# Lending two PSUM banks to the convolution inside a saturated TensorE stream

## The chip, the cores and the metric

The kernel runs on one core of one Trainium2 chip, as one launch. The metric is the device time of that launch in microseconds, lower is better. Five engines work side by side, each through its own queue in order: PE (TensorE, the matmuls), DVE (VectorE), ACT (ScalarE), POOL (GpSimd) and SP (which here only issues DMAs). Matmul results land in PSUM, which has eight banks of 128 partitions x 512 float32; ACT or DVE must copy a result out before the bank is filled again.

## The reference

What is computed is the forward pass and all gradients of a sum of two branches on a normalised input. Cut to what matters:

```python
x  = A_q                       # 1 x 2048 x 1024, bf16
xn = layernorm(x)
# branch A: short convolution of k (4 taps), times v, long convolution over
# 2048 steps with ssm_k by FFT of length 4096, plus kv * ssm_D, times q = xn
# branch B: h = relu(xn @ W_gate) * (xn @ W_up);  out = h @ W_down   (F = 3584)
out = x + A(xn, k, v, shift_k, ssm_k, ssm_D) + B(xn, W_gate, W_up, W_down)
# outputs: out, and by vjp with grad_out: the gradients of q, k, v, shift_k,
# ssm_k, ssm_D, W_gate, W_up, W_down
```

## The kernel before

Branch B is all dense 128x128 matmuls with 512 columns, and they come in three stages:

1. *hidden*: for each half of the rows and each block of 512 columns of F, per row tile a gate product (`ps_g`), an up product (`ps_u`) and a gradient product (`ps_h`), 8 matmuls each, into one bank each.
2. *weight gradients*: `grad_down` (`ps_d`) and `grad_in` (`ps_w`), 16 matmuls to a product.
3. *output*: `ps_o`, `ps_x` and a rest `ps_r`.

Branch A, the convolution, is done for eight groups of 128 channels. Its FFT is split into small matmuls on tiles of 32x64 or 64x32 of the array, and their passes are put between the dense products of stages 1 and 2. A generator of steps, `slots`, says what each slot holds: a pass on PE (left) and a piece of DVE work (right). Every pass writes tiles of two banks each, from a pool of two tiles, and ACT copies each tile to SBUF (`act`).

```python
self.ps = self.pool("a_ps", 2, space=PSUM)          # branch A: 2 tiles of 2 banks

def fwd2(self, F, half):                             # 64x32 step, filter
    for j0 in range(0, 4, 2):
        for j in range(j0, j0 + 2):
            ps = self.ps.tile([P, 2, 2, 2, 2, 64], F32, name="ps2", tag="aps")
            ...                                      # 32 matmuls of 128 columns
            self.act(F[:, 2 * j:2 * j + 2]..., ps[:]...)
        yield                                        # a pass: two tiles

def fwd2_pair(self):                                 # 64x32 step, both spectra
    for j in range(4):
        ps = [self.ps.tile(...) for _ in range(2)]
        ...                                          # 32 matmuls of 256 columns
        yield                                        # a pass: two tiles

SLOT, DENSE = 1900, (1900, 1250)
A_START = 45_000
# cut: slots(); in it, for one group
#   yield f2, None  x4, with a slot without a pass between them
#   ... yield f2H, tg ; yield f2H, fly ; yield self.inv_b(st, "yt", 0), flh ...
```

Branch B has the other four banks. Each product takes the next of four one-bank tiles:

```python
self.ps = tc.alloc_tile_pool(name="b_ps", bufs=4, space=PSUM)

def ps_tile(self, name):
    return self.ps.tile([P, 512], F32, name=name, tag="bps")

# hidden: who empties the bank
def gate(s, held=False):
    ps = self.ps_tile("ps_g"); self.gemm8(ps, xT[s], wg)
    nc.scalar.activation(out=ru[s][:, 0, :], in_=ps[:], func=ACT.Relu)
def up(s, mid=None, after={}, put=..., hold=False):
    ps = self.ps_tile("ps_u"); self.gemm8(ps, xT[s], wu, mid, after)
    def masked():
        nc.vector.scalar_tensor_tensor(out=ru[s][:, 1, :], in0=ru[s][:, 0, :],
                                       scalar=0.0, in1=ps[:], ...)
    ...
def grad_row(s, mid=None):
    ps = self.ps_tile("ps_h"); self.gemm8(ps, gT[s], wd, mid)
    nc.scalar.copy(out=gh[:], in_=ps[:])

# first rows: up(0) is broken off after 4 matmuls for the rows 1 to 3,
# and its masked() is held back until the middle of up(2)
gate(0); up(0, None, {3: first_mid}, lambda *fs: held.extend(fs), True)

# weight gradients: one product of 16 matmuls
def gemm16(self, ps, lhsT, rhs):
    for st in range(self.ST):
        matmul(ps[:], lhsT=lhsT(st), rhs=rhs(st), start=(st == 0), stop=(st == self.ST - 1))
        if st % 8 == 7:
            yield 1730                               # a slot of branch A may come here
            self.tick()
# and after it: nc.scalar.copy(out=wo[0][:, ob, :], in_=ps[:])
```

Three times in stage 2 four products are open at once (`four`: the first blocks of `grad_down` and `grad_in` and one late in `grad_down`), which takes all four banks.

Of the kernel before, what the change touches and what calls it, by code (L numbers as in the profile page):

```python
# [17 lines left out]
P = 128  # L18
# [27 lines left out]
NB1 = 32  # L46


class ABranch:
# [5 lines left out]
    def __init__(self, tc, pri, S, D, k, v, g, shift_k, ssm_k, ssm_D, xn_d, y_d, sk_d, out_gk, out_gv, out_gsk,  # L55
                 out_gh, out_gsD):
        assert S == 2048 and D % P == 0
        self.tc, self.nc, self.pri = tc, tc.nc, pri
        self.S, self.D, self.NG = S, D, D // P
        self.k, self.v, self.g, self.shift_k, self.ssm_k, self.ssm_D = k, v, g, shift_k, ssm_k, ssm_D  # L60
        self.xn_d, self.y_d, self.sk_d = xn_d, y_d, sk_d
        self.out_gk, self.out_gv, self.out_gsk, self.out_gh, self.out_gsD = out_gk, out_gv, out_gsk, out_gh, out_gsD
        self.pools, self.pin, self.dense, self.queue = [], False, False, []

    def pool(self, name, bufs, **kw):
        p = self.tc.alloc_tile_pool(name=name, bufs=bufs, **kw)
        self.pools.append(p)
        return p

# [260 lines left out]
    def fwd1_filter(self, st):  # L330

        B, hn = self.Bh, st["hn"]
        for k in range(2):
            for x in range(2):
                ps = self.ps.tile([P, 2, 512], F32, name="ps0", tag="aps")
                for b in range(2):
                    rows = slice(64 * x + 32 * b, 64 * x + 32 * b + 32)
                    for h in range(2):
                        self.mm(ps[64 * h:64 * h + 64, b], self.R[rows].rearrange("p a l -> p (a l)"),
                                hn[rows, h, 16 * k:16 * k + 16, :].rearrange("p c n -> p (c n)"))  # L340
                self.act(B[:, :, x, 8 * k:8 * k + 8],
                         ps[:].rearrange("p b (cp i n) -> p b cp n i", i=2, n=NB1))
            yield
# [7 lines left out]
    def fwd1(self, B, src):  # L351
        for r0 in range(0, 16, 8):
            for u in range(2):
                ps = self.ps.tile([P, 2, 8, 64], F32, name="ps1", tag="aps")
                for b in range(2):
                    rows = slice(64 * u + 32 * b, 64 * u + 32 * b + 32)
                    for h in range(2):
                        self.mm(ps[64 * h:64 * h + 64, b], self.R[rows].rearrange("p a l -> p (a l)"),
                                src[rows, r0:r0 + 8, 64 * h:64 * h + 64])
                self.act(B[:, :, :, u, r0:r0 + 8, :], ps[:].rearrange("p b r (cp i) -> p b cp r i", i=2))  # L360
            yield

    def fwd2(self, F, half):
        Bf = self.flp[:, half]
        for j0 in range(0, 4, 2):
            for j in range(j0, j0 + 2):
                ps = self.ps.tile([P, 2, 2, 2, 2, 64], F32, name="ps2", tag="aps")
                for ri in range(2):
                    for m in range(2):
                        for q in range(4):  # L370
                            for e in range(2):
                                rows, l = slice(64 * e, 64 * e + 64), 8 * q + 2 * j + m
                                self.mm(ps[32 * q:32 * q + 32, e, :, ri, m, :], self.FW[rows, l, ri, :],
                                        Bf[rows, l, :].rearrange("p (b c) -> p b c", b=2))
                self.act(F[:, 2 * j:2 * j + 2].rearrange("p e b i c -> p (e b i c)"),
                         ps[:].rearrange("p e b i m c -> p (e b i m c)"))
            yield

    def fwd2_pair(self):

        for j in range(4):
            ps = [self.ps.tile([P, 2, 2, 2, 2, 64], F32, name="ps2", tag="aps") for _ in range(2)]
            for m in range(2):
                for ri in range(2):
                    for q in range(4):
                        for e in range(2):
                            rows, l = slice(64 * e, 64 * e + 64), 8 * q + 2 * j + m
                            self.mm(ps[e][32 * q:32 * q + 32, m, :, :, ri, :], self.FW[rows, l, ri, :],
                                    self.flp[rows, :, l, :].rearrange("p k (b c) -> p b k c", b=2))
            for e in range(2):  # L390
                self.act(self.GK[:, 2 * j + e].rearrange("p b k i (m c) -> p (b k i) m c", m=2),
                         ps[e][:].rearrange("p m b k i c -> p (b k i) m c"))
            yield

# [26 lines left out]
    def inv_a(self):  # L421
        C, Q = self.Cg, self.GKV
        for j0 in range(0, 4, 2):
            ps = [self.ps.tile([P, 2, 2, 2, 2, 64], F32, name="ps3", tag="aps") for _ in range(2)]
            for j in range(2):
                for m in range(2):
                    for ri in range(2):
                        for q in range(4):
                            for e in range(2):
                                rows, x = slice(32 * q, 32 * q + 32), 2 * (j0 + j) + m  # L430
                                self.mm(ps[q // 2][64 * e:64 * e + 64, q % 2, j, m],
                                        self.IA[rows, x, ri].rearrange("p a n -> p (a n)"),
                                        Q[rows, 2 * (j0 + j) + e, :, ri, 64 * m:64 * m + 64],
                                        start=ri == 0, stop=ri == 1)
            for h in range(2):
                self.act(C[:, :, 2 * h:2 * h + 2, 2 * j0:2 * j0 + 4, :],
                         ps[h][:].rearrange("p q j m b (cp i) -> p (b cp) q (j m) i", i=2))
            yield

    def inv_a_pair(self):  # L440

        for j in range(4):
            ps = [self.ps.tile([P, 2, 2, 2, 2, 64], F32, name="ps3", tag="aps") for _ in range(2)]
# [9 lines left out]
            for h in range(2):  # L453
                self.act(self.Cs[:, :, 2 * h:2 * h + 2, 2 * j:2 * j + 2, :],
                         ps[h][:].rearrange("p q m k b (cp i) -> p (k b cp) q m i", i=2))
            yield

    def inv_b(self, st, key, half):
        dst, Cf = self.ttile(key), self.flp[:, half]
        st[key] = dst  # L460
        for j in range(2):
            ps = self.ps.tile([P, 2, 8, 64], F32, name="ps4", tag="aps")
            for q in range(4):
                for e in range(2):
# [4 lines left out]
                     ps[:].rearrange("p h r c -> p r h c"))  # L469
        yield  # L470

    def inv_b_chan(self, st, half):
# [3 lines left out]
        for n0 in range(0, NB1, 16):  # L476
            ps = self.ps.tile([P, 16, 64], F32, name="ps5", tag="aps")
            for n in range(16):
                self.mm(ps[:, n, :], Cf[:, n0 + n, :], self.RB[:].rearrange("p h n -> p (h n)"))
            self.act(dv[:, :, n0:n0 + 16], ps[:].rearrange("p n2 n1 -> p n1 n2"))  # L480
# [17 lines left out]
    def tap_sums(self, st):  # L498

        gks, kp = st["gks"], st["kp"]  # L500
        ps = self.ps.tile([P, 2, 512], F32, name="ps6", tag="aps")
        pd = ps[:, 0, 0:P].rearrange("p (i c) -> p i c", i=4)
# [11 lines left out]
    def both(self, *fs):  # L514
# [3 lines left out]
        return go  # L518

# [11 lines left out]
    def steps(self):  # L531
# [25 lines left out]
        for st in self.sts:  # L557
            for p, d in self.slots(st, st["gi"]):
                self.run(p)
# [198 lines left out]

    def small_outputs(self):
# [17 lines left out]
A_START = 45_000  # L777


class LnMlp:  # L780
# [7 lines left out]
    def open_left(self):  # L788
# [6 lines left out]
        self.ps = tc.alloc_tile_pool(name="b_ps", bufs=4, space=bass.MemoryType.PSUM)  # L795
# [38 lines left out]
    def ps_tile(self, name):  # L834
        return self.ps.tile([P, 512], F32, name=name, tag="bps")
# [184 lines left out]
    def flip_xn(self, st):  # L1020
        xT = self.act_tile("xnT", st)
        h = self.DT // 2 if st < 3 else self.DT
        for k0 in range(0, self.DT, h):
            pst = self.ps.tile([P, self.DT, P], BF16, name="pst_x", tag="bps")
# [21 lines left out]
    def hidden(self, first, goT, load, ln, tables, Wg, Wu, Wd, g, xn_d, h_d, ug_d):  # L1046
# [6 lines left out]
        for n in range(N):  # L1053
# [43 lines left out]
            def up(s, mid=None, after={}, put=lambda *fs: [f() for f in fs], hold=False):  # L1097
                ps = self.ps_tile("ps_u")
# [22 lines left out]
            def first_rows():  # L1121
# [16 lines left out]
                def last_mid():  # L1138
                    flip(4)
                    for f in held[0:2]:  # L1140
                        f()
                    chunk(1)
# [174 lines left out]
    def gemm16(self, ps, lhsT, rhs):  # L1317
        for st in range(self.ST):
            self.pri.pin(self.nc.tensor.matmul(ps[:], lhsT=lhsT(st), rhs=rhs(st), start=(st == 0),  # L1319
                                               stop=(st == self.ST - 1)))  # L1320
            if st % 8 == 7:
# [41 lines left out]
    def grad_down(self, xn_d, ug_d, h_d, out_wd):  # L1363
# [9 lines left out]
        for fb in range(self.FB):  # L1373
# [5 lines left out]
            for j in range(4):  # L1379
                self.pri.now()  # L1380
                if j - 1 in whole:
                    continue
                if j in whole:
                    wo = [self.e2_tile("wo") for _ in range(2)]
                    yield from self.four("ps_d", lambda i, st: hs(st)[:, (j + i // 2) * P:(j + i // 2 + 1) * P],
                                         lambda i, st: gn[st][:, i % 2 * 512:i % 2 * 512 + 512],
                                         lambda i: wo[i // 2][:, i % 2, :], load_xn if fb else none)
                else:
                    wo = [self.e2_tile("wo")]
                    for ob in range(2):  # L1390
                        ps = self.ps_tile("ps_d")
                        yield from self.gemm16(ps, lambda st: hs(st)[:, j * P:(j + 1) * P],
                                               lambda st: gn[st][:, ob * 512:ob * 512 + 512])
                        self.pri.pin(nc.scalar.copy(out=wo[0][:, ob, :], in_=ps[:]))
# [8 lines left out]
    def grad_in(self, ug_d, out_wg, out_wu):  # L1403
        nc, xn, nxt = self.nc, self.xn_nat, self.ugs
        turns = [(fb, w) for fb in range(self.FB) for w in (1, 0)]
        for k, (fb, w) in enumerate(turns):
# [3 lines left out]
            for dp in range(self.DT // 2):  # L1410
# [6 lines left out]
                if k == 0 and dp == 0:  # L1417
                    wo = [self.e2_tile("wi") for _ in range(2)]
                    yield from self.four("ps_w", lambda i, st: xn[st][:, i * P:(i + 1) * P], lambda i, st: sl(st),
                                         lambda i: wo[i // 2][:, i % 2, :], lambda st: None)  # L1420
                else:
                    wo = [self.e2_tile("wi")]
                    for d in range(2):
                        dc = 2 * dp + d
                        ps = self.ps_tile("ps_w")
                        yield from self.gemm16(ps, lambda st: xn[st][:, dc * P:(dc + 1) * P], sl)
                        self.pri.pin(nc.scalar.copy(out=wo[0][:, d, :], in_=ps[:]))
# [90 lines left out]
    def grad_x(self, x, g, xn_d, y_d, h_d, ug_d, Wd, out0, out1):  # L1518
# [57 lines left out]
        self.p_w5.release()  # L1576
        self.ps.release()
# [4 lines left out]
def kernel(  # L1582
# [42 lines left out]
    a.identA = b.ident  # L1625
# [20 lines left out]
    if True:  # L1646
        for a.dense, phase in mlp():
            for ns in phase:
                left -= ns
                while a_steps is not None and left <= 0:  # L1650
                    d = next(a_steps, None)
                    if d is None:
                        a.close()
                        a_steps = None
# [37 lines left out]
```

## Time and profile before

| what | value |
|---|---|
| time, median of three | 1880.54 us (1879.9 to 1881.15) |
| span of the profiled execution | 1878.0 us |
| PE busy | 1853.2 us, 99% of the span |
| DVE busy | 1049.4 us, 56% |
| ACT busy | 609.2 us, 32% |
| granted TensorE clock | 1.0 throughout |

By stage, from the busy time in windows: from 100 to 610 us (*hidden*) DVE is busy 414.71 of 510 us and ACT 233.12; from 610 to 1294 us (nearly all of it *weight gradients*) DVE 416.62 and ACT 288.46 of 684 us; from 1294 us on (*output*) DVE 153.78 and ACT 24.89 of 584 us. PE is busy over 98% in each.

Busy times of PE are not the whole story: matmuls overlap each other, and a pass of the convolution that costs more than its columns still counts as busy. The places to look are the starts of successive groups in PE's order of time, and for each bank how long after its last matmul the engine that empties it is done.

### The profile page before, as it was taken

The numbers are of one execution on the slowest core, as the hardware profiler recorded it, in microseconds if no ns is written. First come the engines' busy times: TensorE is split into PE (matmuls) and PEld (weight loads), VectorE is DVE, ScalarE is ACT, GpSimd is POOL, SyncE is SP. The second block draws the span as 40 slices with busy tenths as digits, with TensorE's granted clock in tenths as the row PEclk, the third lists the DMA queues.
The fourth block names the chain that finished last, engine by engine and source line by source line (L and its number), as shares of the span: only waits on it lengthen the run. The fifth ranks groups of instructions, "written<-read, shape, count | busy, mean of one in ns | idle before, by whom it ended". The sixth has DMA issues, their size and how long they took to land.

```text
span 1878.0 us, 32498 instructions
## 1 busy us (share of the span) xinstructions
PE 1853.2 (99%) x13472; PEld 852.1 (45%) x13707; DVE 1049.4 (56%) x1537; ACT 609.2 (32%) x847; POOL 14.8 (1%) x37
## 2 busy tenths in 40 slices
PE   9999999999999999999999999999999999999999
PEld 4444444444444444444444444444444544444444
DVE  6676986888689686575775856600222222222222
ACT  5755354434534445444444454320000000000000
POOL 1000000000000000000000000000000000000000
PEclk9999999999999999999999999999999999999999
DMA  9897589697577765376564452596999955555553
GB/s 255 255 239 171 141 204 234 168 210 176 142 174 218 224 146 167 91 197 193 144 151 138 118 164 74 152 257 171 234 270 241 241 119 124 124 123 124 124 123 73
DMA packets 695509, 323.72 MB, mean 172 GB/s; under 512 B 524864, under 2 KB 664896, under 8 KB 695360
## 3 DMA queue, kind: packets, MB, share of 16 engines
q1 hardware_dynamic: 684864, 300.78, 65.2%
q10 hardware_dynamic: 9216, 16.65, 2.7%
q0 software_dynamic: 1280, 4.20, 0.6%
q8 instruction: 107, 1.75, 0.4%
q14 instruction: 42, 0.34, 0.1%
HBM read 143.79 MB, written 95.44 MB: 127 GB/s over the span
## 4 chain that ended last, share of the span: by engine, by line
PE 97%; issue 1%; DVE 1%; DMA 0%; ACT 0%; SPq 0%; DVEq 0%; ACTq 0%
PE ps_x L1550 20%; PE ps_w L1319 20%; PE ps_h L987 10%; PE ps_u L987 10%; PE ps_g L987 10%; PE ps_o L1481 10%; PE ps_d L1319 9%; PE ps L72 5%; PE ps_d L1332 1%; PE ps_w L1332 1%; PE ps_r L1511 0%; SPq L1005 0%; DMA ug_d<-ru 0%; DMA ln_x<-in_A_q_dram 0%; DVE ln_bn L900 0%
## 5 line engine op out<-in xcount | busy, mean ns | idle before, releaser
L1319 PE MATMUL ps_w<-ugs,xn_nat 128*128 128x512 bf16 x1669 | 376.6, 379 | 5.2 <-issue 3.2
L76 ACT CAST arena<-ps 128x1024 bf16<-128x1024 f32 x288 | 277.7, 1018 | 170.7 <-PE ps L72 162.3
L987 PEld LDWEIGHTS <-xnT 128*128 128x128 bf16 x1792 | 170.6, 98 | 209.5 <-issue 9.8
L1319 PEld LDWEIGHTS <-xn_nat 128*128 128x128 bf16 x1728 | 164.3, 98 | 201.3 <-issue 10.2
L327 DVE STREAM_TRANSPOSE arena<-arena 128x1024 f32<-128x1024 f32 x96 | 180.3, 1933 | 118.7 <-ACT arena L76 117.2
L987 PE MATMUL ps_u<-wu,xnT 128*128 128x512 bf16 x867 | 204.1, 379 | 2.1 <-issue 0.8
L987 PE MATMUL ps_h<-wdT,goT 128*128 128x512 bf16 x867 | 202.6, 379 | 2.7 <-issue 1.1
L987 PE MATMUL ps_g<-wg,xnT 128*128 128x512 bf16 x867 | 202.9, 379 | 2.2 <-issue 0.5
L1568 ACT ACTIVATE w<-xn,m 128x512 f32<-128x512 bf16 x32 | 24.3, 806 | 553.3 <-issue 317.5
L1550 PE MATMUL ps_x<-wuT,guT 128*128 128x512 bf16 x878 | 197.5, 379 | 1.0
L1550 PE MATMUL ps_x<-wgT,ggT 128*128 128x512 bf16 x878 | 197.3, 379 | 0.9
L1481 PE MATMUL ps_o<-wd,hT 128*128 128x512 bf16 (+1 forms) x879 | 186.7, 372 | 0.9
L1319 PE MATMUL ps_d<-g_nat,hs 128*128 128x512 bf16 x739 | 167.9, 379 | 2.9 <-issue 2.1
L1550 PEld LDWEIGHTS <-guT 128*128 128x128 bf16 x896 | 87.7, 98 | 105.7
L1550 PEld LDWEIGHTS <-ggT 128*128 128x128 bf16 x896 | 87.7, 98 | 105.5
L1481 PEld LDWEIGHTS <-hT 128*128 128x128 bf16 x896 | 87.7, 98 | 100.0
L987 PEld LDWEIGHTS <-goT 128*128 128x128 bf16 x896 | 85.5, 98 | 104.5 <-issue 4.7
L1552 DVE CUSTOM_DVE_ANT_0 gx<-ps_x,gy 128x512 f32<-128x512 f32 x32 | 22.1, 692 | 184.2 <-PE ps_x L1550 182.4
L1229 ACT CAST gh<-ps_h 128x512 bf16<-128x512 f32 x112 | 65.7, 586 | 179.3 <-PE ps_h L987 175.0
L1102 DVE SCALAR_TENSOR_TENSOR ru<-ru,ps_u 128x512 bf16<-128x512 bf16 x112 | 76.5, 683 | 80.7 <-PE ps_u L987 48.2
L1473 DVE TENSOR_TENSOR ya<-ya,xe 128x1024 bf16<-128x1024 bf16 x16 | 11.1, 693 | 193.3 <-DMA xe<-xn_d 193.3
L80 DVE TENSOR_TENSOR t<-arena 128x2048 bf16<-128x2048 bf16 x96 | 113.9, 1220 | 0.4
(152 smaller groups left out, 1320.3 us busy)
## 6 DMA issues: line engine op xcount, KB each, us to landing
ug_d<-ru SPq DMA_DIRECT2D x112, 256.0 KB
ugs<-ug_d SPq DMA_DIRECT2D x112, 256.0 KB
wg<-in_B_W_gate_dram SPq DMA_DIRECT2D x56, 256.0 KB
wu<-in_B_W_up_dram SPq DMA_DIRECT2D x56, 256.0 KB
h_d<-ht SPq DMA_DIRECT2D x112, 128.0 KB
hs<-h_d SPq DMA_DIRECT2D x56, 256.0 KB
out_dram<-wi SPq DMA_DIRECT2D x56, 256.0 KB
gt<-in_grad_out_dram SPq DMA_DIRECT2D x32, 256.0 KB
```

What stands on the lines that cost most here:

```text
L72: self.pri.pin(self.nc.tensor.matmul(out, lhsT=lhsT, rhs=rhs, start=start, stop=stop))
L76: self.pri.pin(self.nc.scalar.copy(out=out, in_=in_))
L80: self.pri.pin(self.nc.vector.tensor_tensor(out=out, in0=in0, in1=in1, op=op))
L327: self.pri.pin(self.nc.vector.transpose(out=df[:, c0:c0 + 32, :], in_=sf[:, c0:c0 + 32, :]))
L987: self.pri.pin(self.nc.tensor.matmul(ps[:], lhsT=xT[:, kt * P:(kt + 1) * P], rhs=w(kt), start=(kt == 0), stop=(kt == self.DT - 1)), always ...
L1102: return self.pri.pin(nc.vector.scalar_tensor_tensor(out=ru[s][:, 1, :], in0=ru[s][:, 0, :], scalar=0.0, in1=ps[:], op0=ALU.is_gt, op1=ALU ...
L1229: self.pri.pin(nc.scalar.copy(out=gh[:], in_=ps[:]))
L1319: self.pri.pin(self.nc.tensor.matmul(ps[:], lhsT=lhsT(st), rhs=rhs(st), start=(st == 0), stop=(st == self.ST - 1)))
L1332: self.pri.pin(self.nc.tensor.matmul(ps[i][:], lhsT=lhsT(i, st), rhs=rhs(i, st), start=(st == 0), stop=(st == self.ST - 1)))
L1481: nc.tensor.matmul(ps, lhsT=hT[:, kt, :], rhs=self.wd[:, kt, oc], start=(kt == 0), stop=(kt == self.FT - 1))
L1550: nc.tensor.matmul(ps, lhsT=T[:, kt, :], rhs=W[:, kt, oc], start=(i == 0), stop=(i == n - 1))
L1568: nc.scalar.activation(out=w[:, oc], in_=xn[:, oc], func=ACT.Identity, scale=m[:, 7:8], bias=m[:, 6:7])
```

## The change

Branch B keeps two one-bank tiles of its own; its other two banks become one tile `lent` of two banks. While `lends` is off, branch B uses the four in turn: own, half 0 of `lent`, own, half 1. While it is on (in stage 2, outside the stretches where four products are open), branch B has its own two only, and branch A may use `lent` as the third of its tiles (`cap` is 3). The steps on 64x32 tiles are cut into single tiles, which stage 2 puts together in passes of three: 3, 3 and 2 for the eight tiles of a group, and 3 and 1 for the four of the filter, the one beside `inv_b`. The eight single tiles of `fwd2_pair` are by `(j, m)`; the matmuls are the same. The ACT copy of a product stands directly behind its last matmul, ahead of the slot that may follow. `A_START`, the point at which branch A begins to be given slots, moves from 45,000 to 60,000 ns. The purpose is fewer passes, and so fewer changes of tile shape on PE.

```diff
+    def banks(self):
+        self.turns += 1
+        if self.cap == 3 and self.turns % 3 == 0:
+            return self.lent[:].rearrange("p a x -> p (a x)")
+        return self.ps.tile([P, 1024], F32, name="ps", tag="aps")[:]
 ...  # every ps tile of branch A now comes from banks()
+    def parts(self, p):           # cuts a slot's list of tiles at cap
+        ...
-            for p, d in self.slots(st, st["gi"]):
-                self.run(p)
+            for p, d in (self.wide_slots if self.dense else self.slots)(st, st["gi"]):
+                *more, last = self.parts(p)
+                for fs in more:
+                    self.all_of(fs)
+                    yield self.DENSE[0]
+                self.all_of(last)
 ...
+    def wide_slots(self, st, gi):
+        f2 = [(1, self.f2_pair(j, m)) for j in range(4) for m in range(2)]
+        if self.cap == 3:
+            yield f2[0:3], None
+            yield None, None
+            yield None, None
+            yield f2[3:6], None
 ...
+        yield f2[6:8], q
 ...
+        yield f2H[0:3], tg
 ...
+        yield f2H[3:4] + [(2, self.inv_b(st, "yt", 0))], tk
 ...
-A_START = 45_000
+A_START = 60_000
 ...
-        self.ps = tc.alloc_tile_pool(name="b_ps", bufs=4, space=bass.MemoryType.PSUM)
+        self.ps = tc.alloc_tile_pool(name="b_ps", bufs=2, space=bass.MemoryType.PSUM)
+        self.p_lent = tc.alloc_tile_pool(name="b_lent", bufs=1, space=bass.MemoryType.PSUM)
+        self.lent = self.p_lent.tile([P, 2, 512], F32, name="lent")
+        self.turns, self.lends, self.kept = 3, False, False
 ...
-    def ps_tile(self, name):
-        return self.ps.tile([P, 512], F32, name=name, tag="bps")
+    def ps_tile(self, name, keep=False):
+        if keep:                              # up(0) of the first rows
+            self.kept = True
+            return self.lent[:, 1, :]
+        self.turns += not self.lends
+        n = self.turns % (3 if self.kept else 4)
+        if self.lends or n in (0, 2):
+            return self.ps.tile([P, 512], F32, name=name, tag="bps")
+        return self.lent[:, n // 2, :]
 ...
-    def gemm16(self, ps, lhsT, rhs):
+    def gemm16(self, ps, lhsT, rhs, out):
 ...
+            if st == self.ST - 1:
+                self.pri.pin(self.nc.scalar.copy(out=out, in_=ps[:]))
             if st % 8 == 7:
                 yield 1730
 ...  # grad_down: cap = 3 after the first product that follows four(); cap = 2 again
 ...  # in its last block; grad_in: lends on, and cap = 3, behind its four()
```

## The prediction

> **What bounds the kernel now.** I read the chain of waits first, then PE's waits, then PE's order of time stage by stage, then how late ACT and DVE empty each bank. The chain is PE almost from end to end:
>
> ```profile
> PE 97%; issue 1%; DVE 1%; DMA 0%; ACT 0%; SPq 0%; DVEq 0%; ACTq 0%
> ```
>
> PE's own waits are next to nothing. The largest entries are changes of tile shape ("issue"), 0.16 us each; ACT appears once:
>
> ```profile
> PE ps_w L1319 <- issue: 3.2, 20, 0.2
> ...
> PE ps_h L987 <- ACT ru L1095: 0.3, 1, 0.3
> ```
>
> So only PE's own work can be shortened, and any new wait of PE lengthens the run one for one. In the weight gradients, PE's order of time (start, length) shows what one pass costs:
>
> ```profile
> 1011.50 3.63 PE L1319 MATMUL ps_w<-ugs,xn_nat 128*128 128x512 bf16 x15
> 1015.06 0.63 PE L72 MATMUL ps<-arena,FW 64*32 64x256 bf16 x32
> 1015.62 3.63 PE L1319 MATMUL ps_w<-ugs,xn_nat 128*128 128x512 bf16 x15
> ```
>
> From dense start to dense start is 4.12 us. Sixteen dense matmuls take 3.46 us (those from 28.12 to 31.58 us, below), 0.216 each, so the pass costs 0.66. Its columns: 32 matmuls x 256 columns over 8 tiles at 0.216/512 us per column = 0.43. The rest, 0.23 us, is paid per pass. Passes of other shapes, taken in the same way, keep 0.22 to 0.24 over their columns; the filter's 64 matmuls of 128 columns cost 1.00.
>
> **What the Trainium skill says.** "TensorEngine Tiling (Array Packing)", Key Properties: changing the tiling mode drains TensorE. The 0.23 us per pass agrees with it. "PSUM — Partial Sum Buffer", PSUM bank collisions: two engines must be kept apart by bank and quadrant. The halves of `lent` are different banks, so the chip asks for no wait between them; what a program adds is another matter. "Perfetto Trace Analysis", Matmuls: independent groups should rotate through different banks so that ACT or DVE empties one during the next. The trace agrees: with four banks PE waits 0.3 us in all for ACT. The same page, Tensor Engine Instruction, calls ACT and DVE strict FIFO: an instruction that empties a bank stands behind whatever is queued ahead of it. The DVE rows below show this.
>
> **Part 1: fewer passes (gain).** Counting runs between dense products in the two built programs: 177 passes before, 171 after. The weight gradients go from 99 to 97 although the later start moves four passes of one group into them from the hidden stage (78 to 74). Four groups save one pass each of their eight tiles, three save one by `inv_b` sharing a pass, and the group that runs with `cap` 2 adds one: net 6. The matmuls are the same 13707. Gain: 6 x 0.23 = 1.4 us, all on the path.
>
> **Part 2: two banks for the weight gradients (about nothing).** A product must be emptied before the next but one starts, one product (3.46 us) after its end. ACT needs:
>
> ```profile
> 1011.63 1.93 ACT L76 CAST arena<-ps 128x1024 bf16<-128x1024 f32 x2 [1.70 <-PE ps L72]
> 1013.45 0.61 ACT L1427 CAST wi<-ps_w 128x512 bf16<-128x512 f32 x1
> ```
>
> Worst case: a pass of three in the middle of a product. Three copies take about 2.9 us; half a product (1.73) runs meanwhile, so the product's copy ends some 2.9 - 1.7 + 0.6 = 1.8 us after it, under 3.46. The copy behind the last product keeps later convolution copies from standing ahead of it. I count 0 to 1 us; hence 0.
>
> **Part 3: `lent` in the hidden stage (loss).** The built program of the change shows what the diff does not: dependencies on `lent` are kept for the whole tile. A product that writes half 0 waits for the reader of half 1, and the reverse, in over 190 places. Before, a bank came back after three other products (3 x 1.73 = 5.2 us). Now every second product waits for the reader of the product two before it: 1.73 us.
>
> *First rows.* These I can follow by hand, as the order is the same up to there:
>
> ```profile
> 7.41 1.90 PE L987 MATMUL ps_g<-wg,xnT 128*128 128x512 bf16 x8
> 9.15 1.03 PE L987 MATMUL ps_u<-wu,xnT 128*128 128x512 bf16 x4
> 10.22 0.62 PE L1026 MATMUL pst_x<-ident,ln_x 128*128 128x128 bf16 x8
> ...
> 17.78 1.03 PE L987 MATMUL ps_u<-wu,xnT 128*128 128x512 bf16 x4
> 18.92 0.61 PE L1026 MATMUL pst_x<-ident,ln_x 128*128 128x128 bf16 x8
> ```
> ```profile
> 9.35 0.60 ACT L1095 ACTIVATE ru<-ps_g 128x512 bf16<-128x512 f32 x1 [0.36 <-PE ps_g L987]
> ```
> ```profile
> 18.19 0.68 DVE L1102 SCALAR_TENSOR_TENSOR ru<-ru,ps_u 128x512 bf16<-128x512 bf16 x1
> ...
> 20.51 0.68 DVE L1102 SCALAR_TENSOR_TENSOR ru<-ru,ps_u 128x512 bf16<-128x512 bf16 x1
> ```
>
> The first gate product, in half 1, waits for two copies instead of one (0.25). The first up product is also put in half 1, behind it: it cannot start at 9.15 but after the Relu ends, 9.95. The transposes move from 10.22 to about 11.1 and the layer norm's chain with them: +0.9. The four up matmuls at 17.78 now need the bank that DVE empties at 18.87, and come ahead of the transposes instead of in their shade: +0.86. The fourth gate product (half 0) waits for the held product of row 0 in half 1 (DVE, 20.51 to 21.19, by now 1.75 later): +0.9. That is 2.7 us by the fourth row.
>
> *Until branch A starts.* ACT has the sums of the layer norm ahead of the Relus:
>
> ```profile
> 28.12 3.62 PE L987 MATMUL ps_g<-wg,xnT 128*128 128x512 bf16 x15
> 31.58 3.62 PE L987 MATMUL ps_u<-wu,xnT 128*128 128x512 bf16 x16
> ```
> ```profile
> 32.76 0.58 ACT L1095 ACTIVATE ru<-ps_g 128x512 bf16<-128x512 f32 x1
> ```
>
> The gate product that ended at 30.02 is emptied at 33.34; two products on, the up product started at 31.58 in another bank. With `lent` it waits 1.8 us. I went through all products to 100 us so, with the bank the change gives each: 1.8 at 31.6, 1.8 at 42.8, 0.2 at 67.8, 1.05 at 74.7, and 0.1 at 24. Sum 4.9; with the first rows 7.6. The one at 42.8 hangs on a DMA and may shrink.
>
> *With branch A.* DVE is the busy one (414.71 of 510 us). An example, PE and then DVE:
>
> ```profile
> 359.98 3.62 PE L987 MATMUL ps_u<-wu,xnT 128*128 128x512 bf16 x16
> 363.43 5.34 PE L987 MATMUL ps_h<-wdT,goT 128*128 128x512 bf16 x23
> ```
> ```profile
> 361.51 1.94 DVE L327 STREAM_TRANSPOSE arena<-arena 128x1024 f32<-128x1024 f32 x1
> ...
> 364.35 1.95 DVE L327 STREAM_TRANSPOSE arena<-arena 128x1024 f32<-128x1024 f32 x1
> 366.15 0.67 DVE L1102 SCALAR_TENSOR_TENSOR ru<-ru,ps_u 128x512 bf16<-128x512 bf16 x1
> ```
>
> The second up product ends near 363.6 and its bank is free at 366.82; the product two on starts at 365.16, harmless before, a wait of 1.7 us if both lie in `lent`. From 100 to 610 us I find 17 such cases, all with an up product, 16.9 us together. Half the products lie in `lent`: 8.5. As a wait of PE lets DVE catch up before the next case, I take 6.
>
> **Part 4: the later start (about nothing).** Branch A ends 88 dense matmuls nearer the end of the weight gradients: 216 remain, 46.7 us. Then `wd` must load; its last piece is queued behind the third last weight store (about 14 us before the stage ends) and used 4.5 us into the next stage. Before, all four pieces were moved within about 25 us, so one has time. The output stage has 6 us per product against DVE copies of 0.7: no wait.
>
> **Sum.** 1880.5 - 1.4 + 0 + 7.6 + 6 = 1892.7; I take 1892, since part of the early waits may be absorbed.
>
> **Rivals.** (a) *Only the passes count*: 1879. For it: the trace has no PE waits to speak of, and the banks are different ones. Against it: the waits are in the built program, and the readers' ends are in the trace. (b) *Waits as above without relief*, each late reader biting and more in the shifted pairing: 1897 to 1902. For it: the shift of branch A's steps against the products is new; against it, only half the products lie in `lent`. (c) *Two banks bind in the weight gradients, or `wd` comes late*: +3 to +10, 1895 to 1902. For it: ACT's worst case leaves 1.6 us; against it, ACT is busy 288 of 684 us there.
>
> **Range and chances.** Below is (a) with little early waiting, 1882; above (b) or a part of (c), 1900. Two per cent are 37.6 us; nothing here comes to that. Faster by over 2%: 0.005, PE's work cannot shrink so far. Slower by over 2%: 0.015. Within: 0.98.
>
> **What would show it.** Right: PE's waits gain entries from ACT `ru` and DVE `ru` for lines of the hidden stage, 10 to 17 us together; the first up product starts near 10.2 us; the stage of the weight gradients is shorter by a microsecond or so. Wrong: no such entries and a time near 1879, which would mean that readers come earlier than I think; or waits for ACT `wi` and `wo`, or for the DMA of `wd`, which would be (c).

## The result, and the profile after

| | before | after |
|---|---|---|
| time, median of six runs | 1880.41 us (1879.9 to 1881.17) | 1888.38 us (1886.89 to 1888.81) |
| span of the profiled execution | 1878.0 us | 1886.7 us |
| PE busy | 1853.2 us, 99% | 1855.7 us, 98% |

The ratio is 1.004, with a 95% interval of 1.0027 to 1.0053: slower by about 8 us, inside the predicted range and 3.6 us under the predicted 1892. The matmuls are the same; PE's busy time is 2.5 us longer, and the mean granted clock is 1.000 before and 0.999 after, since one short stretch runs at half clock (below). The rest of the time went into waits of PE, and the chain of waits of the changed kernel shows that it is no longer PE alone:

```profile
PE 93%; issue 3%; DVE 3%; ACT 1%; DMA 0%; POOL 0%; DVEq 0%; POOLq 0%; ACTq 0%
```

PE's waits in the changed kernel follow (what waited and its line, for whom: us in all, times, longest):

```profile
PE lent L1171 <- DVE ru L1286: 4.8, 5, 2.2
PE lent L1171 <- ACT ru L1279: 2.6, 3, 1.6
PE ps_w L1504 <- issue: 2.4, 15, 0.2
...
PE lent L1171 <- DVE xnT L1215: 1.2, 3, 0.6
...
PE lent L1171 <- ACT gh L1414: 0.8, 1, 0.8
...
PE ps_u L1171 <- DVE ru L1286: 0.2, 1, 0.2
```

L1171 is the dense matmul of the hidden stage. Nearly every new wait there is before a product into `lent`; before one into an own bank there is 0.2 us (`ps_u`). The main readers are those that the prediction named, ACT `ru` and DVE `ru`, 7.6 us together. ACT `gh` and DVE `xnT` (0.3 us before) add 2.0 that it did not name.

The rows "issue" are not waits, here or in the kernel before. Both traces lack some records of matmuls: 13472 and 13478 of 13707 are there. Each entry of these rows lies at a change of shape and is 0.22 to 0.23 us, the length of one matmul, longer than the same change of shape in a trace that has all records. The traces of the experiments have all 13707, and none has such a row.

To see where the time came and went, I compared the start of the same dense matmul in both traces, at the ends of the stages. These are differences after minus before, in us:

| dense matmul | before at | difference |
|---|---|---|
| first | 7.41 | +0.24 |
| number 300, shortly before branch A's passes begin in earnest | 77.24 | +5.52 |
| first of the weight gradients | 644.06 | +10.31 |
| first of the output stage | 1294.10 | +8.76 |
| number 8000, near the end | 1854.47 | +8.76 |

The hidden stage lost 10.3 us, the weight gradients gave back 1.55, and the output stage changed nothing. The first rows, in PE's order of time, went as the prediction had worked them out by hand:

```profile
10.22 1.02 PE L1171 MATMUL lent<-wu,xnT 128*128 128x512 bf16 x4 [0.69 <-ACT ru L1279]
11.09 0.61 PE L1210 MATMUL pst_x<-ident,ln_x 128*128 128x128 bf16 x8
...
36.19 1.89 PE L1171 MATMUL lent<-wu,xnT 128*128 128x512 bf16 x8 [1.65 <-ACT ru L1279]
```

The first up product starts at 10.22 (9.15 before; predicted "near 10.2"), the transposes at 11.09 (predicted 11.1). The wait that was foreseen at 31.6 us of the kernel before is the one at 36.19, 1.65 us long. With branch A the largest wait is this one; first PE, then DVE:

```profile
391.71 1.89 PE L1171 MATMUL ps_u<-wu,xnT 128*128 128x512 bf16 x8
395.84 3.53 PE L1171 MATMUL lent<-wdT,goT 128*128 128x512 bf16 x8 [2.24 <-DVE ru L1286]
399.30 0.63 PE L80 MATMUL ps<-arena,RB 64*32 64x512 bf16 x16
```
```profile
390.23 3.71 DVE L335 STREAM_TRANSPOSE arena<-arena 128x1024 f32<-128x1024 f32 x2
...
395.11 0.68 DVE L1286 SCALAR_TENSOR_TENSOR ru<-ru,lent 128x512 bf16<-128x512 bf16 x1
```

The up product into `lent` ended near 391.9, but DVE, which takes its work in order, had two transposes and two products of branch A (the lines left out) ahead of it and read the bank at 395.11 to 395.79. PE starts 395.84, in the *other* half of `lent`. From 391.71 to 395.84 are 4.13 us where a product takes 1.73, so the wait costs 2.40; the 2.24 in the bracket is a little less, as the modelled end of the last matmul reaches beyond the start that the next would have had.

This wait costs more than itself. The product behind it takes 3.46 us from its start to that of the pass behind it, twice 1.73, and the busy times of windows show why; the number behind the busy times of the five engines is the granted clock:

```profile
391.00:395.80 4.80, 2.60 (x12) 1.07 (x11) 4.75 (x5) 0.00 (x0) 0.00 (x0) 1.00 0.17 55
395.80:399.20 3.40, 3.36 (x8) 0.99 (x7) 2.65 (x5) 0.00 (x0) 0.00 (x0) 0.50 0.23 77
```

The stretch at half clock is 3.41 us long, so it loses 1.7 us. The traces of the kernel before, the changed kernel and the ten experiments have, between the first dense product and the last, eight waits of PE of 2.08 us or more, and at each of them a stretch at half clock begins, from 0.8 us before the wait's end to 1.2 us after it. Eight waits of 1.6 to 1.8 us have none, and neither has a trace without a longer wait. That the wait brings about the lower clock is read from this company alone; no experiment set a wait's length.

### The profile page after: what moved, and what is told of

Same layout as the page of the kernel before. It is cut to its first block, busy times and chain, and to the rows that moved or that the text cites. A ratio compares the mean times of both kernels' runs of the same rounds, so it can differ in the third digit from the quotient of the medians.

```text
span 1886.7 us, 32515 instructions
## 1 busy us (share of the span) xinstructions
PE 1855.7 (98%) x13478; PEld 852.8 (45%) x13707; DVE 1051.7 (56%) x1537; ACT 610.2 (32%) x847; POOL 14.8 (1%) x37
## 4 chain that ended last, share of the span: by engine, by line
PE 93%; issue 3%; DVE 3%; ACT 1%; DMA 0%; POOL 0%; DVEq 0%; POOLq 0%; ACTq 0%
PE ps_w L1504 19%; PE lent L1171 13%; PE ps_x L1744 10%; PE lent L1744 10%; PE ps_d L1504 9%; PE ps_o L1675 5%; PE lent L1675 5%; PE ps_g L1171 4%; PE ps L80 4%; PE ps_h L1171 4%; PE ps_u L1171 4%; PE lent L1504 1%; PE lent L1519 1%; PE lent L80 1%; PE ps_d L1519 1%
## 5 line engine op out<-in xcount | busy, mean ns | idle before, releaser
L1171 PEld LDWEIGHTS <-xnT 128*128 128x128 bf16 x1792 | 171.0, 98 | 214.9 <-issue 14.4
L84 ACT CAST arena<-ps 128x1024 bf16<-128x1024 f32 x240 | 233.9, 1019 | 72.3 <-PE ps L80 62.6
L1171 PEld LDWEIGHTS <-goT 128*128 128x128 bf16 x896 | 85.8, 98 | 111.2 <-issue 13.0
L1507 ACT CAST wi<-ps_w 128x512 bf16<-128x512 f32 x101 | 59.5, 589 | 182.1 <-PE ps_w L1504 151.8
L1504 PEld LDWEIGHTS <-hs 128*128 128x128 bf16 x768 | 72.6, 98 | 89.4 <-issue 5.5
L1171 PE MATMUL lent<-wdT,goT 128*128 128x512 bf16 x432 | 106.4, 384 | 5.1 <-DVE ru L1286 4.0
L1171 PE MATMUL lent<-wg,xnT 128*128 128x512 bf16 x445 | 107.1, 379 | 2.8 <-DVE ru L1286 0.8
L1171 PE MATMUL ps_u<-wu,xnT 128*128 128x512 bf16 x445 | 106.7, 379 | 1.3 <-issue 0.6
L1667 DVE TENSOR_TENSOR ya<-ya,xe 128x1024 bf16<-128x1024 bf16 x16 | 11.1, 692 | 173.6 <-DMA xe<-xn_d 173.6
L1171 PE MATMUL lent<-wu,xnT 128*128 128x512 bf16 x430 | 103.7, 379 | 3.8 <-ACT ru L1279 2.6
L1171 PE MATMUL ps_h<-wdT,goT 128*128 128x512 bf16 x430 | 104.5, 379 | 1.2 <-issue 0.5
L1171 PE MATMUL ps_g<-wg,xnT 128*128 128x512 bf16 x422 | 102.1, 379 | 1.3 <-issue 0.6
L1415 DVE TENSOR_TENSOR ru<-ru,gh 128x1024 bf16<-128x1024 bf16 x112 | 76.9, 688 | 46.8 <-ACT gh L1414 46.6
```

Source lines behind the costliest of these rows:

```text
L84: self.pri.pin(self.nc.scalar.copy(out=out, in_=in_))
L1171: self.pri.pin(self.nc.tensor.matmul(ps[:], lhsT=xT[:, kt * P:(kt + 1) * P], rhs=w(kt), start=(kt == 0), stop=(kt == self.DT - 1)), always ...
L1415: self.pri.pin(nc.vector.tensor_tensor(out=ru[s][:], in0=ru[s][:], in1=gh[:].rearrange("p (o f) -> p o f", o=1).to_broadcast([P, 2, 512]), ...
L1507: self.pri.pin(self.nc.scalar.copy(out=out, in_=ps[:]))
```

## The experiments

The theory: the scheduler keeps dependencies for the tile `lent` as a whole, so products into its two halves wait for each other's readers. That costs some 11 us in the hidden stage, while the third tile of the convolution gains about 3 us. The rivals: the later start of branch A, the place of the copies, passes of three tiles, or the rotation of banks as such. "Before" in each comparison is the kernel before, run on the same chip (medians 1880.0 to 1880.8).

### Four own banks in the hidden stage

```diff
-        self.ps = tc.alloc_tile_pool(name="b_ps", bufs=2, space=PSUM)
-        self.p_lent = ...; self.lent = self.p_lent.tile([P, 2, 512], F32, name="lent")
+        self.ps = tc.alloc_tile_pool(name="b_ps", bufs=4, space=PSUM, side="right")
 ...  # ps_tile(): always from self.ps until the weight gradients begin; there:
+        self.ps.release()
+        self.ps = alloc_tile_pool(name="b_ps2", bufs=2, ...)
+        self.p_lent = ...; self.branch.lent = self.lent = ...
```

> The changed kernel, but its hidden stage has the four one-bank tiles that it had before the change; the two-bank tile `lent` takes the place of two of them only where the weight gradients begin. Theory (the scheduler keeps dependencies for `lent` as a whole, so in the hidden stage its two halves wait for each other): the waits of TensorE for ACT ru and DVE ru in the hidden stage, some 11 us by the trace, go; the early rows run as before; the gain of the weight gradients (about 2 us fewer waits and 1.3 us of passes) stays, so the time is about 1877 us, 11 below the changed kernel and 3 below the kernel before. Rival (the loss comes from the later start of branch A, from the copies behind the last product or from the three-tile passes): the time stays near 1888.

Measured 1885.83 us, ratio to before 1.0029 (1.002 to 1.0039). Neither number. By starts of the same matmuls the hidden stage came back to that of the kernel before (-0.14 us at the first matmul of the weight gradients, where the changed kernel has +10.31) and the output stage began 0.99 us early, as the theory wants. Then the output stage lost 10.9 us, which it does not lose in the changed kernel. This view of PE's waits says where:

```profile
PE lent L1678 <- DVE o L1680: 8.1, 5, 3.9
```

L1678 is the product of the output stage (`ps_o`). So the theory held for the hidden stage, and the run had found a second place of the same kind, for which I had no explanation yet. The longest of these waits, 3.9 us, has a stretch at half clock behind it (1.7 us). The profiled execution took 1889.62 us, 3.8 above the median, so most executions lose less there than 10.9.

### `lent` alone, in the kernel before

```diff
-        self.ps = tc.alloc_tile_pool(name="b_ps", bufs=4, space=PSUM)
+        self.ps = tc.alloc_tile_pool(name="b_ps", bufs=2, space=PSUM)
+        self.p_lent = tc.alloc_tile_pool(name="b_lent", bufs=1, space=PSUM)
+        self.lent = self.p_lent.tile([P, 2, 512], F32, name="lent")
 ...  # ps_tile() takes own, half 0, own, half 1 in turn, to the end; no lending
```

> The kernel before, with one thing of the change alone: of the four one-bank tiles two are the halves of one two-bank tile `lent`, used in the rotation of the change. Nothing is lent to the convolution, branch A starts as before, its steps and the output copies are those of before. Theory (whole-tile dependencies): 1890 to 1892 us, 10 to 12 above the kernel before, with waits of TensorE for ACT ru and DVE ru in the hidden stage; as nothing is given back in the weight gradients, it should be a little slower than the changed kernel. Rival (the loss has another cause): 1880.

Measured 1903.76 us, 1.0122 (1.0109 to 1.0135): 12 us above the expected range. The hidden stage lost 11.7 us by the starts of the same matmuls, as expected; 0.3 more went in the weight gradients, and again the output stage lost 10.3, of which 1.7 are a stretch at half clock behind the wait of 4.8. PE's waits:

```profile
PE lent L1492 <- DVE o L1494: 7.8, 4, 4.8
PE lent L997 <- DVE ru L1112: 5.8, 6, 1.5
PE lent L997 <- ACT ru L1105: 2.3, 2, 1.6
```

### The same, with the two banks as two tiles

```diff
-        self.lent = self.p_lent.tile([P, 2, 512], F32, name="lent")
+        self.lent = [self.p_lent.tile([P, 512], F32, name=f"lent{i}") for i in range(2)]
```

> The kernel of the run with `lent` alone, but the two lent banks are two tiles of one bank each; order of use, banks and everything else are the same. Theory (the loss is due to the two halves being one tile for the scheduler's dependencies, not to the fixed rotation or to the banks): 1880 us, as before, and the waits for ACT ru and DVE ru are gone. Rival (the rotation itself, or the chip's two banks side by side, costs the time): 1890, as with the one tile.

Measured 1881.47 us, 1.0005 (0.9997 to 1.0013). Same rotation, same banks, same instructions, and 22 us less than with one tile of two banks. PE's waits:

```profile
PE ps_u L997 <- DVE ru L1112: 1.0, 1, 1.0
PE lent L997 <- ACT ru L1105: 0.7, 1, 0.7
```

Both losses are gone, in the hidden stage and in the output stage. What stays is 1.3 us from the first rows: the first up product is put into the very bank of the first gate product and waits for its Relu (0.7), and while it holds that bank only three are left to rotate (1.0). This run settles the cause: it is the tile's size in the program's dependencies. Beyond these 1.3 us neither the rotation nor the chip's banks cost the time.

### No third tile

```diff
-                            self.branch.cap = 3      # in grad_down and in grad_in
+                            self.branch.cap = 2
```

> The changed kernel, but the convolution never gets the third tile: its passes hold two tiles at most and `lent` lies idle in the weight gradients, while the dense products there still have two banks. Theory (the third tile spares six passes of 0.23 us and about 2 us of waits for the evictions of the two-tile pool): 1891 to 1892 us, 3 above the changed kernel. Rival (the third tile does nothing for the time, or its passes cost as much as they spare): 1888, as the changed kernel; and if two banks bind the dense products there, waits before ps_w and ps_d appear.

Measured 1913.11 us, 1.0171 (1.0158 to 1.0184), over 20 us above both expectations. The weight gradients did as the theory says: they lost 2.4 us against before where the changed kernel gains 1.55, a difference of 3.9. The other 22 us went in the output stage, 14 of them in two rows of the waits:

```profile
PE lent L1675 <- DVE o L1677: 9.3, 6, 2.9
PE lent L1675 <- DMA wd<-in_B_W_down_dram: 5.0, 2, 3.9
```

The DVE waits are the ones met above. The DMA is new: with fewer tiles to a pass branch A's last copies began only at 1274 us (1222 before, 1250 in the changed kernel), the loads of `wd` begin after that, and PE reached the first product before the last of them. Three stretches at half clock, 13.7 us together, stand beside the three waits of 2.08 us or more in that stage. They lose another 6.4 us, as 0.8 us of them falls into a wait; with 0.16 us more for each of the eight listed waits the 22 are accounted for. So the third tile also pays for the later start, and this run cannot price it alone.

### `lent` in the weight gradients only

```diff
 ...  # four own banks in the hidden stage, as above; and at the start of the output stage:
+        self.p_lent.release(); self.ps.release()
+        self.ps = tc.alloc_tile_pool(name="b_ps3", bufs=4, space=PSUM, side="right")
```

> The changed kernel with the two-bank tile `lent` in the weight gradients alone: four one-bank tiles in the hidden stage, as in the run with four own tiles there, and four again from the output stage on. That run lost 10.9 us in the output stage, all of it before products into `lent` that waited for the addition (DVE o) of the row block before. Theory (the dependencies on `lent` as a whole are the cause there too): these waits go, the output stage starts about 1 us earlier than in the kernel before and keeps that, so about 1879 us, 1 below the kernel before and 9 below the changed kernel. Rival (the output stage lost its time to late transfers, the later start of branch A and of the load of wd behind it): the waits stay with another name, 1885 to 1890.

Measured 1878.83 us, 0.9994 (0.9986 to 1.0003): the expected 1879. The waits for DVE `o` are gone with the tile. Against this run, which has the same passes and the same start of branch A, the changed kernel is 10.31 + 1.18 = 11.5 us late at the first matmul of the weight gradients. But at that border this run itself pays for its change of pools, and again ahead of the output stage:

```profile
PE ps_d L1517 <- ACT gh L1412: 0.7, 1, 0.7
PE ps_o L1682 <- ACT wi L1505: 0.7, 1, 0.7
```

Each is 0.84 us by the starts. At the last product of the hidden stage, ahead of both, the difference is 654.15 - 641.82 = 12.3 us. That is what `lent` costs there, the stretch at half clock included.

### The turn shifted by one in the output stage

```diff
         nc, tc, D = self.nc, self.tc, self.D
         self.pri.now()
+        self.turns += 1
         p_ev = tc.alloc_tile_pool(name="o_ev", bufs=2, side="right")
```

> The changed kernel with one count added to the turn of the tiles at the start of the output stage, and nothing else: there the first half of every row of 128 tokens now falls to `lent` and the second to the two own banks, where the changed kernel has it the other way round. Theory (in the output stage the changed kernel has the same whole-tile dependencies, and escapes the waits only since the half that meets the late addition of x and y first lies in an own bank): waits of TensorE for DVE o in the output stage, as in the two runs that had this order, and 1896 to 1899 us, 8 to 11 above the changed kernel. Rival (those runs lost their time there for another reason): 1888, as the changed kernel.

Measured 1898.42 us, 1.01 (1.0086 to 1.0113), inside the expected range: 10 us more than the changed kernel for one count. First DVE and then PE in this run, and after them DVE in the changed kernel:

```profile
1364.94 0.69 DVE L1669 TENSOR_TENSOR ya<-ya,xr 128x1024 bf16<-128x1024 bf16 x1 [3.97 <-DMA xr<-in_A_q_dram]
1365.74 0.69 DVE L1678 TENSOR_TENSOR o<-lent,ya 128x512 bf16<-128x512 f32 x1
```
```profile
1352.62 6.21 PE L1676 MATMUL lent<-wd,hT 128*128 128x512 bf16 x28
1358.67 6.21 PE L1676 MATMUL ps_o<-wd,hT 128*128 128x512 bf16 x28
1366.48 6.20 PE L1676 MATMUL lent<-wd,hT 128*128 128x512 bf16 x28 [1.61 <-DVE o L1678]
```
```profile
1377.19 0.69 DVE L1668 TENSOR_TENSOR ya<-ya,xr 128x1024 bf16<-128x1024 bf16 x1 [3.21 <-DMA xr<-in_A_q_dram]
1377.99 0.69 DVE L1677 TENSOR_TENSOR o<-ps_o,ya 128x512 bf16<-128x512 f32 x1
1378.59 0.68 DVE L1677 TENSOR_TENSOR o<-lent,ya 128x512 bf16<-128x512 f32 x1
```

Each row of 128 tokens has two products of 6.05 us and needs `ya`, the sum of other inputs, for both additions. `ya` waits for loads and comes late, after both products are done or nearly so. The addition of the first product is then a whole product late, that of the second is in time. If the first product lies in `lent`, the next product into `lent` follows one product later and waits (at 1366.48). If the second does, as in the changed kernel, there is a product in between: the addition at 1378.59 to 1379.27 is before 1381.42, when the next product into `lent` starts. So the changed kernel has the same dependency in the output stage and escapes by the parity of a counter; the runs with four own banks in the hidden stage, with `lent` alone and without the third tile had the other parity.

### Branch A's start as before

```diff
-A_START = 60_000
+A_START = 45_000     # with lent in the weight gradients only
```

> The run with `lent` in the weight gradients alone, with branch A's start as in the kernel before (45,000 in place of 60,000 of its own measure). Theory (the later start costs and brings next to nothing while branch A still ends early enough for the load of wd): within 2 us of that run, about 1879. Rival (the later start was paid for in waits of TensorE on a second stream that has less time): 1876 or below. A third possibility, that the later start spares passes of the convolution: 1881 or above.

Measured 1878.38 us, 0.9991 (0.9985 to 0.9998). The later start is worth nothing either way as long as `wd` is in time. The hidden stage has four passes more again and the weight gradients three fewer, which shifts 1.6 us between the stages and leaves the sum.

### The same without the third tile

```diff
-                            self.branch.cap = 3
+                            self.branch.cap = 2
```

> As the run before it (branch A at 45,000, `lent` in the weight gradients alone), but the convolution never gets `lent`: its passes hold two tiles at most. Theory (the third tile spares six passes of 0.23 us and about 2 us of waits for the evictions of its two tiles): 3 us more than that run, about 1882, and waits before ps_w or ps_d return in the weight gradients. Rival (the third tile brings nothing, and the gain there was that of the steps' new order): within 1 us of that run.

Measured 1882.03 us, 1.001 (1.0002 to 1.0018): 3.65 us more, near the expected 3. Passes in the weight gradients are 94 with the third tile and 102 without: eight, not six, so 8 x 0.23 = 1.8 us. Five waits of passes come back, of 0.24 to 0.38 us by the starts, 1.5 us together. A further 1.2 us at 873 are a DMA's (`xn_nat`), which another execution may not have. What such a wait looks like is seen in the kernel before, first PE and then ACT:

```profile
819.91 0.30 PE L72 MATMUL ps<-arena,IA 32*64 32x256 bf16 x4
820.50 0.63 PE L72 MATMUL ps<-arena,IA 32*64 32x256 bf16 x28 [0.29 <-ACT arena L76]
```
```profile
818.53 1.93 ACT L76 CAST arena<-ps 128x1024 bf16<-128x1024 f32 x2 [2.05 <-PE ps L72]
```

The pass before it left two tiles to ACT at 818.5; the second is copied only at 820.46, and the new pass, which may do four matmuls in the first tile, stands still for the other 28. A third tile removes just this.

### The copies behind branch A's step again

```diff
-            if st == self.ST - 1:
-                self.pri.pin(self.nc.scalar.copy(out=out, in_=ps[:]))
             if st % 8 == 7:
                 yield 1730
                 self.tick()
+        self.pri.pin(self.nc.scalar.copy(out=out, in_=ps[:]))
```

> The run with `lent` in the weight gradients alone and branch A at 45,000 (1878.4 us), but the copy of each finished weight-gradient product stands where it stood before the change: behind the step of branch A that is taken after the product, so behind that step's evictions on ScalarE. Theory (with two banks the product after next waits for the copy; it has 3.46 us from the end of one product to the end of the next, and up to three evictions of 1.02 us may now stand ahead of a copy of 0.59 us): waits of TensorE for ACT wi or ACT wo in the weight gradients, 1 to 4 us in all, so 1879.5 to 1882.5. Rival (the evictions leave room, the copy's place doesn't matter): within 0.7 us of 1878.4.

Measured 1879.13 us, 0.9991 (0.9983 to 0.9999), against 1878.38. This theory fell. The weight gradients take the same time in both traces to 0.01 us (2.14 and 2.15 us less than in the kernel before), and no wait for `wi` or `wo` is new; the small difference arises before that stage. Between two products ACT has room for the copies in either place.

### The best version

```diff
 ...  # four own banks in the hidden stage, A_START 45_000, lent to the end; and
         self.pri.now()
+        self.turns = 3       # first half of a row in an own bank, second in lent
         p_ev = tc.alloc_tile_pool(name="o_ev", bufs=2, side="right")
```

> Four one-bank tiles in the hidden stage, branch A at 45,000, `lent` from the weight gradients to the end as in the changed kernel, and the turn set so that the first half of every row in the output stage falls to an own bank and the second to `lent`. There is no change of pools ahead of the output stage, which cost 0.84 us in the run with `lent` in the weight gradients alone. Theory (in this order the whole-tile dependencies cost nothing in the output stage, as in the changed kernel): 1877.5 us, 3 below the kernel before, and no wait for DVE o. Rival (the second half waits as well once nothing else has slowed TensorE): some waits for DVE o, 1880 or above.

Measured 1877.83 us, 0.9985 (0.9978 to 0.9991): near the expected 1877.5 and 2.96 us under the kernel before on the same chip. Against the run with four own banks in both other stages and the same start (0.9991, 0.9985 to 0.9998) the intervals overlap. PE's chain is whole again, and among its waits none is for DVE `o` or `ru`:

```profile
PE 99%; DVE 0%; ACT 0%; issue 0%; POOL 0%; POOLq 0%
```

## Why the prediction was right

**Part 3, the loss in the hidden stage, carried it.** Predicted 13.6 us, measured 12.3 (against the run with `lent` in the weight gradients only). The early part was put at 7.6 and is 5.6: the wait of 1.8 at 42.8 us, of which the text said that it hangs on a DMA and may shrink, did not come, and nearly all others did at their size. With branch A 6 was taken. Five waits there cost 4.9 us by the starts of the same matmuls, and the stretch at half clock behind the longest adds 1.7, which the text did not foresee: it took a wait of PE to lengthen the run one for one. So the size was partly luck: half of 16.9 us was cut to 6 by a guess, and the waits are five and unlike, the largest 2.40 us. One named sign failed: the listed waits for ACT `ru` and DVE `ru` are 7.6 us, not 10 to 17. The mechanism is shown, not argued: the same two banks as two tiles cost next to nothing.

**Part 1, fewer passes, 1.4 us,** stands by its count (177 to 171). The 0.23 us of a pass was taken from starts of matmuls and does not hang on the rows "issue", which the text took for changes of tile shape. No run changes the number of passes alone.

**Part 2, two banks for the weight gradients, 0,** was too small a view of a right statement. Two banks do suffice for the dense products of the changed kernel, and the copies' place is indifferent, which the prediction had left at "0 to 1 us". But it asked only what the change takes from the dense products. In the kernel before the passes themselves waited for ACT now and then, since two tiles of a pass had to be copied before the next pass could finish. The text said that ACT appears once among PE's waits; the same view has a second row:

```profile
PE ps L72 <- ACT arena L76: 0.3, 1, 0.3
```

By the starts of matmuls within a pass its weight gradients have nine such waits, of 0.24 to 0.58 us, 2.75 us together, and each ends 0.05 us after an ACT copy. All but one are too short for the view, which counts from a matmul's modelled end. With the third tile none is left. They are the term that the sum lacked.

**Part 4, later start about nothing,** was right for the start itself (1878.38 and 1878.83 us with either). For the output stage its reason was wrong. "6 us per product against DVE copies of 0.7: no wait" counts the length of the addition and not when it can begin. The addition waits for loads and is often a product late. That it costs the changed kernel nothing is a matter of parity, as 10 us for one count show.

**The sum.** By the traces, 5.5 (the table's +5.52) and 4.9 of waits and 1.7 of half clock in the hidden stage, 2.75 less in the weight gradients and 1.4 less for passes make 7.95 us. The medians differ by 7.97 and the two profiled executions by 8.76, so up to 0.8 us I could not assign. Beside the prediction's 12.2, the early part and the waits with branch A are 3.2 us smaller and the passes' own waits take off 2.75, while the half clock puts on 1.7: errors of both signs make up the 3.6 us by which the time stayed under 1892 and the 0.7 that were rounded off there.

**The rivals.** (a), only the passes count, has the number that the change would have had with one-bank tiles outside the weight gradients, 1878 to 1879, but not its reason alone: the passes' own waits are in it too. (b) and (c) did not come, though (c), late `wd`, is real: without the third tile the later start brings it about.

## What to carry to other kernels

A bank that is joined with another into one tile may lose its independence: count the tiles whose dependencies are kept apart, and not the banks, when asking how long a reader may be late. When buffers shrink from four to two in effect, look at every stage that uses them for when the reader can begin (what else it waits for, what stands ahead of it in its queue), and not for how long it takes. A stage that shows no wait may be right by the parity of a counter only; shift the counter by one to learn whether it is. Behind a long wait, look at the granted clock as well: here each wait of 2.08 us or more stood beside a stretch at half clock that cost another 1.4 us or more.

## What the runs showed that I had not expected

- The output stage leans on its four banks all the time. From 1310 to 1880 us DVE waits 124.5 us for the load of `xe` in the kernel before and 123.8 in the changed one, and PE for nothing in either. One engine's idle time of this size is harmless only as long as the banks bridge it.
- Changing pools of PSUM tiles ahead of the output stage costs 0.84 us by the starts of the matmuls on both sides, in all four runs that do it, and nothing where the old pool goes on: the first product of the new pool waits for ACT's copy of the last one of the old. The best version does without it there, and begins its output stage 0.7 us earlier than the run with the pools changed and the same start of branch A.
